# A fused attention and gMLP block on one core: a prologue written out as one order, z2's normalisation dealt out anew among the engines, weights split earlier, and loads paced

## The chip, the cores and the metric

The kernel runs on one core of one Trainium2 chip. A core has five engines with a queue of instructions each: TensorE (PE: matrix products; PEld is its loading of weights), VectorE (DVE), ScalarE (ACT: functions of one argument, such as exp, tanh, square, copy), GpSimd (POOL) and SyncE (SP), which here only issues DMA transfers. Data lie in SBUF (128 partitions) and in PSUM, where TensorE writes. An engine takes the instructions of its queue in order; engines wait for each other through semaphores. The metric is device time in microseconds, the median of several runs.

## The reference

With x of 2048 x 512 and xn = layernorm(x):

```
A:  q, k, v = split(xn @ wqkv)             # 32 heads of 16
    p = softmax(q k^T / 4);  A = concat(p v) @ wo
B:  z  = gelu(xn @ w_in)                   # 2048 x 1792, tanh form
    z1 = z[:, :896];  z2 = layernorm(z[:, 896:])
    g  = w_sp @ z2 + b_sp[:, None]         # w_sp: 2048 x 2048
    B  = (z1 * g) @ w_out
out = x + A + B
```

All is float32. The softmax is exact, with each query's maximum taken off before the exponential.

## The kernel before, in words

**Products.** Dense products are made of three passes in the format fp32r: each operand is split into a high part (a rounded copy) and a low part (the rest), and hi x hi, lo x hi and hi x lo are summed in PSUM. Splitting is a copy (ScalarE or GpSimd) and a subtraction (VectorE or GpSimd). In the main loop a dense slot is a pair of matmuls on the two halves of the array's rows, into the two halves of the PSUM tile `dps`; three further PSUM tiles, `sl[0..2]`, serve the attention and are handed out by `take`.

**Attention.** The 32 heads go in 16 pairs (p), each with 4 groups of 512 queries (c) and 16 tiles of keys (kt): 1024 steps. Each step has a scores product `scores` (L1157), an exponential on ScalarE (`exp`, tile `pf`, 8 buffers), and its part of the product with v (`values`, L1258, in bursts of 8 steps, so 128 bursts). The maxima come from a product of their own, `maxima` (L1171), whose rows VectorE reduces (`max_red`, L872, tile `mm`). After 16 of them, `max_fin` writes the negated maxima through DRAM (`mscr`) into two extra rows of the stacked q (`qst`), so that the scores product itself takes them off. The scores of a group can't start before its 16 maxima have come back. v lies in `vall`; `v_rest` makes its tiles 4 to 15 in pairs.

**The written order and the planner.** The whole program is one instruction stream per engine, written by a planner in Python that keeps a clock for each engine (`T`) with estimated durations. The main loop goes through the strings of `ORDER`: S scores, M maxima, D dense slot, V a burst of values; one string is one cycle and has 24 D. The dense work is a queue of generators: `v_rest`, `qk_rest` (q and k of head groups 1 to 3), `z2_all` (16 tiles), `z1_all` (14 pairs), `spatial` (28 units of 48 slots), `mlp_out`, `attn_out`. After each pair or tile, a "q" holds the queue until the next burst (`hold`), if more than 8 slots were spent. If nothing else can be done, `filler` (L1230) multiplies zeros. Work of ScalarE, VectorE and GpSimd off the main chain is made of tasks with a priority; those of priority 2 on ScalarE and VectorE run inside a window, the time of the burst, or when older than `AGE`. The list `late` holds DMA issues with due times. `room` counts free buffers; of the tag "big" there are 19 tiles of 512 KB.

**The prologue** (before the main loop, L1043 to L1086) is written group by group of 512 rows of x: `norm_x` (statistics on VectorE, L341; scale, L344 to L346; applied by GpSimd, L350), `turn_x` (transposes on TensorE, L356, split by `split`, L242), `qk_first` (q and k of the first four head pairs, L245 to L247, split and stored, then reloaded as stacks by `load_stacks`), and `v_tile` for four tiles of v. The first weights come twice, once by SP for the subtraction (L268) and once by GpSimd's queue as the high part (L262). v's weights are split by GpSimd (L270, L271). Transposed x is stored to `xscr` by GpSimd's queue: groups 0 and 1 in the prologue (L164), 2 and 3 in the main loop (from L158, from `XAT` on, `XBY` apart). The first maxima come after the prologue, once the planner's clock is past `FIRST`.

**z2** (`z2_norm`, L511): per tile of 128 x 896, ScalarE squares (a gelu in tanh form), GpSimd scales (L518) and multiplies (L520), ScalarE takes tanh, GpSimd adds 1 (L524) and multiplies by z (L526), VectorE takes the statistics (two of 448, L533, and one aggregate, L535), GpSimd forms the scale from them (L539 to L544, one column each) and applies it in two parts, hi and lo (L550 to L554), and SP stores them to `z2scr`.

**Weights ahead.** `weight` loads a weight, waits, and splits it on GpSimd (L291, L293). `ahead_of_time` does that for the 7 weights of z1 and 8 of the spatial product and stores the parts to DRAM (`w1scr`, `wsscr`), from where `fetch_parts` brings them back when needed. Both are spawned in `qk_rest`. `z_loader` brings z2's parts for the spatial product.

## Time and profile before

| | us |
|---|---|
| median of 3 runs (lowest, highest) | 1856.94 (1855.68, 1857.37) |
| the profiled execution | 1855.84 |
| its span, first to last instruction | 1853.9 |
| TensorE busy | 1807.5 (97%) |
| VectorE busy | 1440.9 (78%) |
| ScalarE busy | 1189.6 (64%) |
| GpSimd busy | 722.0 (39%) |
| first dense slot of the main loop | 64.91 |
| first scores product | 102.70 |
| first burst of values | 114.70 |

The profile is one execution, taken by the hardware profiler. A row of its timeline has a start, a duration, the engine, the line of the kernel, the operation, what it writes and reads, a count, and in brackets how long the engine had been idle and who released it. Rows of the same kind that follow each other are merged. Matmuls overlap, so the time from one start to the next tells what one costs, not its duration. A group row gives the count, the total busy time, the mean in ns of one, and the idle time before the group's instructions. POOL's spans are rough.

### The profile page before, as it was taken

What the parts mean: (1) busy time and instruction counts of PE and PEld (TensorE: products, weight loads), DVE (VectorE), ACT (ScalarE), POOL (GpSimd) and SP (SyncE); (2) the same over time, 40 slices, a digit from 0 to 9 for tenths busy, and PEclk for the clock granted to TensorE, in tenths of its full rate; (3) what the DMA queues carried; (4) which work ended last, traced back from release to release, by engine and by line L of the source; (5) the groups of instructions that cost most, each with busy time, mean ns of one, the idle gap of its engine ahead of it and who ended that gap; (6) DMA issues with size and microseconds to landing.
All of it is one profiled execution on the core that took longest, in us unless ns stands there. A gap on an engine that the chain in (4) does not pass through costs nothing.

```text
span 1853.9 us, 38030 instructions
## 1 busy us (share of the span) xinstructions
PE 1807.5 (97%) x14778; PEld 1093.5 (59%) x14778; DVE 1440.9 (78%) x1677; ACT 1189.6 (64%) x1292; POOL 722.0 (39%) x808
## 2 busy tenths in 40 slices
PE   6999999999999999999999999999999999999998
PEld 4766566655655565556556665666656556565543
DVE  6578778888888787877878787787778878787883
ACT  2157777687776777666666665666656666565665
POOL 5324342778888777222452135102522240002200
PEclk9999999999999999999999999999999999999999
DMA  7728872533565246656867558565767667575422
GB/s 236 288 93 283 277 238 87 127 91 112 133 217 137 100 119 201 152 160 154 219 171 199 156 180 217 155 146 154 194 164 186 177 173 148 149 175 143 130 86 80
DMA packets 212124, 306.14 MB, mean 165 GB/s; under 512 B 36816, under 2 KB 108048, under 8 KB 209056
## 3 DMA queue, kind: packets, MB, share of 16 engines
q1 hardware_dynamic: 202824, 273.83, 53.8%
q0 software_dynamic: 9120, 29.89, 4.7%
q8 instruction: 116, 1.90, 0.4%
q14 instruction: 64, 0.52, 0.1%
HBM read 193.80 MB, written 109.85 MB: 164 GB/s over the span
## 4 chain that ended last, share of the span: by engine, by line
PE 87%; DVE 5%; DMA 2%; ACT 2%; issue 1%; POOL 1%; SPq 1%; DVEq 0%; ACTq 0%; POOLq 0%
PE dps L1216 35%; PE sl L1258 23%; PE sl L1157 14%; PE sl L1171 12%; DVE mm L872 3%; SPq L134 1%; PE dps L1230 1%; ACT pf L78 1%; DMA zs<-z2scr 1%; POOL wsp L293 0%; DMA wsp_11r<-in_w_spT 0%; PE sl L247 0%; PE sl L246 0%; PE sl L245 0%; PE sl L1016 0%
## 5 line engine op out<-in xcount | busy, mean ns | idle before, releaser
L872 DVE TENSOR_REDUCE mm<-sl 128x2 f32<-128x1024 f32 x1024 | 1223.8, 1222 | 202.2 <-PE sl L1171 195.8
L78 ACT ACTIVATE pf<-sl 128x1024 f32<-128x1024 f32 x1024 | 1041.6, 1026 | 335.1 <-PE sl L1157 298.5
L1258 PE MATMUL sl<-pf,vall 128*32 128x512 f32 x4096 | 467.9, 595 | 1.0 <-DVE on L1006 0.6
L1157 PE MATMUL sl<-qst,kst 50*128 50x512 f32 x2048 | 436.0, 418 | 9.4 <-DVE mm L872 2.9
L1171 PE MATMUL sl<-kst,qst 48*128 48x512 f32 x2048 | 422.1, 405 | 4.5 <-DVE mm L872 2.4
L1216 PE MATMUL dps<-wsp,zs 64*128 64x512 f32 x2352 | 379.0, 392 | 1.6 <-DMA zs<-z2scr 1.5
L1157 PEld LDWEIGHTS sl<-qst,kst 50*128 50x128 f32 x2048 | 194.3, 184 | 221.9 <-issue 79.6
L1258 PEld LDWEIGHTS sl<-pf,vall 128*32 128x32 f32 x4096 | 119.3, 109 | 266.9 <-issue 234.3
L1171 PEld LDWEIGHTS sl<-kst,qst 48*128 48x128 f32 x2048 | 195.1, 185 | 105.0 <-ACT pf L78 52.6
L1216 PEld LDWEIGHTS dps<-wsp,zs 64*128 64x128 f32 x2352 | 226.9, 187 | 39.3 <-DMA zs<-z2scr 2.2
L78 ACT ACTIVATE e<-sl 128x512 f32<-128x512 f32 x64 | 38.3, 598 | 205.2 <-PE sl L1258 198.0
L1280 DVE TENSOR_TENSOR e<-sl,e 128x512 f32<-128x512 f32 x64 | 44.3, 692 | 134.3 <-PE sl L1258 76.3
L778 POOL TENSOR_TENSOR hhl<-z1i,hhl 128x512 fp32r<-128x512 f32 x28 | 36.1, 1297 | 267.1 <-ACT hhl L78 267.0
L1216 PE MATMUL dps<-w,xt 64*128 64x448 f32 x768 | 110.4, 368 | 1.5
L1216 PE MATMUL dps<-wout,hp 64*128 64x512 f32 x672 | 110.5, 393 | 0.0
L923 POOL TENSOR_TENSOR ob<-ob 128x512 f32<-128x512 f32 (+1 forms) x16 | 20.6, 1285 | 195.2 <-DMA ob<-rscr 195.2
L1216 PEld LDWEIGHTS dps<-w,xt 64*128 64x128 f32 x768 | 73.5, 186 | 16.3 <-issue 7.8
L1216 PEld LDWEIGHTS dps<-wout,hp 64*128 64x128 f32 x672 | 65.8, 187 | 9.2
L919 POOL TENSOR_TENSOR ob<-ob 128x512 f32<-128x512 f32 (+1 forms) x16 | 20.6, 1287 | 101.6 <-DMA ob<-escr 100.9
L443 POOL TENSOR_TENSOR qkhl<-qr,qkhl 128x512 fp32r<-128x512 f32 x24 | 30.3, 1282 | 70.4 <-ACT qkhl L78 66.3
L1216 PE MATMUL dps<-wf,zs 64*128 64x512 f32 x336 | 55.5, 393 | 0.1
L1216 PE MATMUL dps<-xnT,wqk 64*128 64x512 f32 x288 | 47.7, 396 | 1.1 <-ACT vall L78 0.4
(289 smaller groups left out, 1688.3 us busy)
## 6 DMA issues: line engine op xcount, KB each, us to landing
zs<-z2scr SPq DMA_DIRECT2D x192, 256.0 KB
escr<-e SPq DMA_DIRECT2D x60, 256.0 KB
hscr<-hhl POOLq DMA_DIRECT2D x28, 512.0 KB, 6.4
qst<-qscr SPq DMA_DIRECT2D x30, 384.0 KB
kst<-kscr SPq DMA_DIRECT2D x30, 384.0 KB
qscr<-qkhl SPq DMA_DIRECT2D x16, 512.0 KB
kscr<-qkhl SPq DMA_DIRECT2D x16, 512.0 KB
xscr<-xnT POOLq DMA_DIRECT2D x16, 512.0 KB, 4.8
```

The costliest lines, as they stand in the source:

```text
L78: return nc.scalar.activation(out, in_, func, **kw)
L134: nc.sync.dma_start(raw(dst), raw(src))
L443: nc.gpsimd.tensor_sub(hl[:, 1, :], raw_, hl[:, 0, :].bitcast(F32))
L778: nc.gpsimd.tensor_sub(hl[:, 1, :], z1, hl[:, 0, :].bitcast(F32))
L872: nc.vector.tensor_reduce(mmax[g][:, :, t, kc], sl[k], AX.X, ALU.max)
L919: nc.gpsimd.tensor_add(both_[rows, 0, :], both_[rows, 0, :], both_[rows, 1, :])
L923: nc.gpsimd.tensor_mul(both_[rows, 0, :], both_[rows, 0, :], both_[rows, 1, :])
L1157: nc.tensor.matmul(sl[k][:, j, :], kst[p % 2][rows, kt * P:(kt + 1) * P], qst[p % 2][rows, c * 512:(c + 1) * 512], start=True, stop=True)
L1171: nc.tensor.matmul(sl[k][:, j, :], qst[p % 2][rows, tt * P:(tt + 1) * P], kst[p % 2][rows, kc * 512:(kc + 1) * 512], start=True, stop=True)
L1216: nc.tensor.matmul(dps[:, bank, :w], lhs, rhs, start=go, stop=stop)
L1258: nc.tensor.matmul(sl[k][cols:cols + VW, 0, :], vpack(kt + r, 2 * p + j), pf[:, j * 512:(j + 1) * 512], start=n % CYC == 0, stop=n % CYC = ...
L1280: nc.vector.tensor_add(e, sl[k][:, 0, :], e)
```

## The change

1. **The prologue is one list of words, `STEPS`,** which the class `First` turns into instructions. Its letters: S statistics, R scale, N apply (a star: the second tile on ScalarE), T transposes, E split of transposed x, Z its store (group 0 only, by SP), WH/WL high and low part of the first weights, Q and F the first q and k (a star: by ScalarE and GpSimd), L load of stacks, B the bias, VH/VL v's weights, V and VE v's first tiles, M and X the first 16 maxima and their reductions. PSUM tiles are handed out in turn (four). The first weights are loaded once and split on the chip; 22 products of zeros (`WARM`) come before the first transposes. The main loop starts with 16 maxima done and `max_fin(0)` spawned; `FIRST` is gone. Groups 1 to 3 of transposed x are stored in the main loop by GpSimd's queue, from 5 us on, 2 us apart.
2. **v's outputs:** of each pair, one is evicted by VectorE instead of ScalarE. The hold after a pair now applies only once all of v is done.
3. **z2:** tanh's +1 and the product with z, with the sum over the row, are one VectorE instruction per half of 448; GpSimd adds the two sums to the negated mean; ScalarE squares z minus its mean with the sum over the row. The statistics, the aggregate and two GpSimd instructions go. `u` is freed after the square. The planner's durations for GpSimd in z2 change.
4. **Weights ahead** are spawned in `v_rest`, at the second pair, all 15 at once, instead of in `qk_rest` in three lots.
5. **Pacing:** `road`, `clear` and `bulk`: a weight load is issued only when the planner's clock has passed the end of the loads before, counted at 1 us each, a fetch of parts or of z2 at 2 us (a z2 part that is needed next goes anyway). x is fetched again for q and k at wider steps (1.5 for 0.5).
6. `AGE` goes from 6 to 9.

```
-FIRST = 7.0
+VAHEAD = 6
-XAT = 8.0
+XAT = 5.0
-AGE = 6.0
+AGE = 9.0
+WARM = 22
+STEPS = (
+    "S00 S01 R00 WH0 N00 WL0 R01 S10 N01* T01 S11 WH1 T03 E03 T00 E01 R10 T02 WL1 E02 E00 R11 N10 N11* Q00 T13 T12 "
+    "T11 F00* S20 VH1* S21 E13 R21 E12 Q01 VH3* T10 N21* S30 R20 E11 E10 Q11 VL1* R30 N20 F01* B VH0 Z03 N30* "
+    "T20 S31 E20 R31 T23 Z02 L0 F11 Z01 E23 N31* Q10 F10 T32 T21 T22 T30 E32 E22 E21 Q20 VH2 L1 T31 VL3 E30 "
+    "T33 Q21 VL0 F20 E31 VL2 M02 E33 M00 Q31 X02 F21 M13 M10 L2 X00 Q30 X13 F31 M03 M01 X10 X03 F30 V3 M22 M12 Z00 "
+    "X01 M23 VE3 X22 V0 VE0 X12 M21 X23 M20 X21 L3 M11 V1 X20 M32 M30 X11 M31 X32 X31 VE1 V2 X30 M33 X33 VE2 "
+)
...
     def weight(out, k, a, spare):
-        yield "C", lambda: raws[0] < DEEP and room["big"] > 1 + spare[0]
+        yield "C", lambda: clear() and raws[0] < DEEP and room["big"] > 1 + spare[0]
+        bulk(1.0)
...
     def fetch_parts(out, k, scr, spare):
-        yield "C", lambda: room["big"] > 1 + spare[0]
+        yield "C", lambda: clear() and room["big"] > 1 + spare[0]
+        bulk(2.0)
...
     def v_out(t, bank):
-        yield "A", ta(512)
-        act(vhead[:, t, :, :DH], dps[:, bank, :].rearrange("p (h d) -> p h d", d=DH), AF.Copy)
+        src = dps[:, bank, :].rearrange("p (h d) -> p h d", d=DH)
+        if bank:
+            yield "D", td(512)
+            nc.vector.tensor_copy(vhead[:, t, :, :DH], src)
+        else:
+            yield "A", ta(512)
+            act(vhead[:, t, :, :DH], src, AF.Copy)
...
+            if t == VAHEAD:
+                for f in range(NF):
+                    owed[0] += 1
+                    spawn(ahead_of_time(f, (f"w1_{f}", w_in[:, f * P:(f + 1) * P], D, ND), w1scr[f], AHEAD), 1)
+                for s in range(KEPT):
+                    owed[0] += 1
+                    spawn(ahead_of_time(s, sp_weights(0, s), wsscr[s], AHEAD), 1)
...
         act(u, u, AF.Tanh, scale=GC)
-        yield "G", 1.2
-        nc.gpsimd.tensor_scalar(u, u, 1.0, 1.0, ALU.add, ALU.mult)
-        yield "G", 2.1
-        nc.gpsimd.tensor_mul(z, u, z)
+        for j, half in enumerate((a, b)):
+            cols = slice(j * 448, (j + 1) * 448)
+            yield "D", 0.63
+            nc.vector.scalar_tensor_tensor(z[:, cols], u[:, cols], 1.0, z[:, cols], ALU.add, ALU.mult, accum_out=half)
+        yield "G", 0.6
+        g.tensor_scalar(m, a, b, -1.0 / FH, ALU.add, ALU.mult)
+        yield "A", ta(FH) + 0.2
+        act(u, z, AF.Square, bias=m, accum_out=square)
         lease("big", 1)
-        for j in range(2):
-            yield "D", 0.62
-            nc.vector.bn_stats(st[:, j, :], z[:, j * 448:(j + 1) * 448])
-        yield "D", 0.1
-        nc.vector.bn_aggr(mv, st)
...
     def z_loader():
         for k in range(len(zparts)):
-            yield "C", lambda: k < zused[0] + 4 and room["big"] > (min(owed[0], ZROOM) if k > zused[0] + 1 and owed[0] else raws[0] > 0)
+            yield "C", lambda: (clear() or k <= zused[0] + 1) and k < zused[0] + 4 and room["big"] > (min(owed[0], ZROOM) if k > zused[0] + 1 and owed[0] else raws[0] > 0)
+            bulk(2.0)
             load_z(k)
...
+        for _ in range(WARM):
+            nc.tensor.matmul(dps[:, 1, :], zeror, brow, start=True, stop=True)
+        first = First(w0r, w0, wvr, wv, braw)
+        for word in STEPS.split():
+            first.step(word)
         steady.append(True)
-        T.update(P=0.0, A=0.0, D=0.0, G=0.0)
+        T.update(P=0.0, A=0.6, D=2.0, G=0.0)
...
-        for g in range(2, NG):
+        for g in range(1, NG):
             for c in range(ND):
-                at(XAT + XBY * (4 * g - 8 + c), nc.gpsimd.dma_start, raw(xscr[g][c]), raw(xnT[g, c]))
+                at(XAT + XBY * (4 * g - 4 + c), keep, g, c)
...
+        spawn(max_fin(0), 0, T["D"])
+        n_st, n_mx, n_pv = 0, 16, 0
...
                 elif it[0] == "q":
-                    hold = spent > 8 and n_pv < N
+                    hold = spent > 8 and n_pv < N and len(vdone) == NT - EARLY
```

More of the change, by code (lines that the diff above doesn't have):

```diff
@@ L247, in mm3, with begin @@
         nc.tensor.matmul(acc, lh, rl, start=False, stop=last)
[L249 removed]
+    def begin(nm, src, n, blocks=1):
         rw = piece(nm + "r").bitcast(F32)[:, 0, :n]
[L253 removed]
+        dst = rw
         if blocks > 1:
@@ L1043, in fused_block @@
         load_x(0)
+        w0r = [begin(*qk_weights(0, a)) for a in range(2)]
         w0 = [piece(f"wqk0_{a}") for a in range(2)]
-        w0r = [begin(*qk_weights(0, a), early=w0[a]) for a in range(2)]
         load_x(1)
@@ L1179, in mx_ok @@
         def mx_ok(t):
-            return n_mx < LEAD and t > FIRST
+            return n_mx < LEAD
         def has_dense(t):
```

240 lines of the change are left out of this document (124 added, 116 removed).

## The prediction

> **What bounds the kernel now.** I read four views in this order: the busy times, stretches by stage, the timeline of the score-times-value bursts (128 of them, one per "cycle"), and the timelines of the opening. The first two, with the group of filler matmuls:
>
> ```profile
> PE 1807.5 (97%) x14778; PEld 1093.5 (59%) x14778; DVE 1440.9 (78%) x1677; ACT 1189.6 (64%) x1292; POOL 722.0 (39%) x808
> ...
> L1230 PE MATMUL dps<-brow,zeror 64*128 64x512 f32 x206 | 39.3, 408 | 0.5 <-ACT z1x L78 0.3
> ...
> 0.00:64.90 64.90, 47.85 (x208) 36.31 (x208) 34.61 (x83) 19.06 (x37) 27.73 (x44) 0.97 0.77 267
> 64.90:133.10 68.20, 63.87 (x516) 44.56 (x516) 50.19 (x52) 24.28 (x30) 23.07 (x29) 1.00 0.42 145
> 133.10:290.70 157.60, 155.17 (x1288) 95.15 (x1286) 126.21 (x141) 116.25 (x134) 63.18 (x62) 1.00 0.78 255
> 290.70:517.30 226.60, 221.42 (x1835) 136.72 (x1834) 187.60 (x232) 166.51 (x185) 161.76 (x190) 1.00 0.42 113
> 517.30:750.70 233.40, 230.17 (x1874) 134.69 (x1874) 186.90 (x215) 167.84 (x190) 183.06 (x214) 1.00 0.50 152
> 750.70:1805.60 1054.90, 1046.77 (x8748) 629.72 (x8748) 839.18 (x935) 670.19 (x690) 263.23 (x270) 1.00 0.64 165
> ```
>
> A row of the second kind is a stretch, its length, then busy time of PE, PEld, DVE, ACT and POOL, clock, DMA share and GB/s. TensorE bounds the kernel. Its idle time is 17.0 us in the opening (64.90 - 47.85), 4.3 in the next stretch, 5.2 in the z2 stage (290 to 517), and 8.1 in the thousand microseconds from 750 on (the spatial stage and the outputs), so there is little to win there. Busy time hides 103 pairs of fillers (206 matmuls of zeros).
>
> ```profile
> 114.70 3.64 PE L1258 MATMUL sl<-pf,vall 128*32 128x512 f32 x32
> 129.51 3.64 PE L1258 MATMUL sl<-pf,vall 128*32 128x512 f32 x32
> 145.04 3.64 PE L1258 MATMUL sl<-pf,vall 128*32 128x512 f32 x32
> ...
> 406.25 3.64 PE L1258 MATMUL sl<-pf,vall 128*32 128x512 f32 x32
> 419.64 3.64 PE L1258 MATMUL sl<-pf,vall 128*32 128x512 f32 x32
> ...
> 517.28 3.64 PE L1258 MATMUL sl<-pf,vall 128*32 128x512 f32 x32
> ...
> 1805.56 2.78 PE L1258 MATMUL sl<-pf,vall 128*32 128x512 f32 x24
> ```
>
> These are the bursts. The second starts at 129.51, the 125th at 1805.56: 123 cycles of 13.63 us. The one from 406.25 ran with no dense work at all, fillers only, and still took 13.39. So a cycle has two limits of the same size, the dense slots on TensorE and the chain of exponentials and maxima. The end therefore sits at "start of the second burst + 126 cycles + tail", as long as the dense pieces keep up with the cycles (a pair or tile of 18 to 24 slots each, one per cycle). The profiled execution took 1855.84 us (span 1853.9); the median of the three runs, 1856.94, is 1.1 above it.
>
> **Part 1, the opening.** Before, TensorE leaves the opening at 64.91, and only then come the first 16 maxima, in 19.62 us of VectorE, and the scores at 102.70:
>
> ```profile
> 4.53 0.69 DVE L341 BATCH_NORM_STATS2 bst<-x 128x6 f32<-128x512 f32 x1 [2.50 <-DMA x<-in_x]
> ...
> 6.05 0.18 DVE L342 BATCH_NORM_AGGREGATE mv<-bst 128x2 f32<-128x6 f32 x1
> 6.60 0.17 DVE L345 RECIPROCAL rs<-rs 128x2 f32<-128x2 f32 x1 [0.36 <-ACT rs L344]
> 6.80 0.16 DVE L346 SCALAR_TENSOR_TENSOR rs<-mv,rs 128x2 f32<-128x2 f32 x1
> ...
> 50.17 1.88 DVE L242 TENSOR_TENSOR xnT<-sl,xnT 128x512 fp32r<-128x512 f32 x3
> ...
> 71.36 19.62 DVE L872 TENSOR_REDUCE mm<-sl 128x2 f32<-128x1024 f32 x17 [8.45 <-PE sl L1171]
> ...
> 48.52 1.04 PE L356 MATMUL sl<-ident,x 128*128 128x128 f32 x8
> ...
> 61.34 0.39 PE L245 MATMUL dps<-qst,xnT 128*128 128x512 f32 x1
> ...
> 63.83 0.39 PE L247 MATMUL dps<-kst,xnT 128*128 128x512 f32 x1
> 64.91 1.43 PE L1216 MATMUL dps<-qst,xnT 64*128 64x512 f32 x10 [0.69 <-ACT vall L78]
> ...
> 102.70 0.41 PE L1157 MATMUL sl<-qst,kst 50*128 50x512 f32 x2
> ...
> 121.22 0.96 PE L1216 MATMUL dps<-xnT,wqk 64*128 64x512 f32 x6 [0.40 <-ACT vall L78]
> ...
> 128.26 1.32 PE L1216 MATMUL dps<-xnT,wqk 64*128 64x512 f32 x10
> ```
>
> After, the written order holds for VectorE: 8 pairs of statistics (4.53 to 6.23, 1.70 each) 13.6; 8 scale steps (6.60 to 6.96) 2.9; 16 low parts of x, 6 of q and k, 2 of the first weights and 3 of v's, 27 of 0.627 (1.88 / 3), 16.9; 16 maxima of 1.154 (19.62 / 17) 18.5; with a small split of the bias, rounded up to 1, together 53. The start at 4.53 is set by the load of x, which stays first in SP's queue, so VectorE is through at 57.5 if it never waits. TensorE has 64 transposes of 0.13 (1.04 / 8), 8.3; 96 + 48 products of 0.227 (63.83 - 61.34 over 11 steps), 32.7; 16 maxima pairs of about 0.23, 3.7: 44.7, from about 10 on, so 55. VectorE is the longer. The 22 warm-up matmuls run while x is on its way, and cost nothing as long as the first normalised halves come later than they end; otherwise at most 22 x 0.227 = 5. The last q and k part must still go out to memory and come back as stacks; maxima of earlier key groups fill that time. I add 5.5 for waits that the order can't hide (ends 0 and 17, the idle time of TensorE in the whole old opening; nearer to 0 because every engine but VectorE has slack here): 16 maxima done at 63 instead of 91. TensorE is free some 1.5 earlier, at 61.5 instead of 64.91, and with 16 maxima already done.
>
> From there to the second burst TensorE took 64.6 us before (64.91 to 129.51). After, some 12 of the 16 maxima pairs are gone from it (12 x 0.227 = 2.7; I let the other four go into running further ahead). So are the q/k products that ran in it: the rows from 121.22 to 128.26 are 46 matmuls, 23 slots of two, 5.2. In the new order no q/k work runs ahead of the second burst, which needs all of v. v's outputs, split between ScalarE and VectorE, may save 1 (ends 0 and 6 x 0.5, one wait like the 0.40 in the row for each pair). That leaves 55.7, so the second burst starts at 117.2: **-12.3**. The 23 slots come back later, in cycles that had fillers. The next cycle, 15.53 before (129.51 to 145.04), should be the mean 13.63: **-2**.
>
> What can eat this is the way of the first maxima to memory and back, for which TensorE waits in its own order:
>
> ```profile
> 122.08 0.61 POOL L291 CAST w<-w_0r 128x512 fp32r<-128x512 f32 x1 [33.97 <-DMA w_0r<-in_w_in]
> ...
> 123.50 1.28 POOL L293 TENSOR_TENSOR w<-w_0r,w 128x512 fp32r<-128x512 f32 x1
> ...
> 184.01 5.82 DMA qst<-mscr
> ...
> 1141.65 10.77 DMA zs<-z2scr
> ...
> 90.00:121.00 31.00, 29.17 (x236) 19.51 (x232) 24.91 (x31) 13.97 (x18) 0.00 (x0) 1.00 0.07 21
> ```
>
> Around 90 to 121 the DMA engines are idle (0.07) and POOL has nothing. The change puts there the 12 stores of x transposed (GpSimd's queue, 2 us apart), 15 weight splits (0.61 + 1.28 us of POOL each) and their loads and stores in SP's queue, where a store that waits for POOL holds up what stands behind it. So the first return of maxima no longer has the road to itself: between 0 and 5.82 (the loaded case above) late; I take **+1**. The same move takes 15 weights out of 133 to 290, where that wait stood in the chain of work that ended last: **-1**.
>
> **Part 2, z2.** Its groups, all in the z2 stretch and a bit beyond:
>
> ```profile
> L526 POOL TENSOR_TENSOR z<-z2u,z 128x896 f32<-128x896 f32 x16 | 33.8, 2110 | 0.3
> ...
> L533 DVE BATCH_NORM_STATS2 zst<-z 128x6 f32<-128x448 f32 x32 | 18.9, 611 | 3.1 <-POOL z L526 3.1
> ...
> L524 POOL TENSOR_SCALAR z2u<-z2u 128x896 f32<-128x896 f32 x16 | 15.0, 940 | 31.7 <-ACT z2u L78 31.5
> L78 ACT ACTIVATE z2u<-z2u 128x896 f32<-128x896 f32 x16 | 15.0, 953 | 3.8 <-POOL z2u L520 3.8
> ```
>
> Per tile POOL loses 2.11 + 0.94 and gains one on a single column: some -2.8. VectorE swaps two statistics (2 x 0.61) and a small aggregate for two products with sums of the same width: even, if nothing holds them up. ScalarE gains one square, 0.95. ScalarE is at 166.5 of 226.6 there and would go to 182; VectorE is at 187.6. POOL is at 161.8 and starts the next stage with a backlog; the cycle from 406.25 without dense work is where it held up new tiles. That cycle's 24 slots are about what the opening pushed back, so I book the relief of POOL against those 23 slots, and the pace of z2 at **0**. Without that cover the 23 slots cost 5.2 at the end.
>
> Against it stands how VectorE and POOL get at the same memory:
>
> ```profile
> 38.63 0.61 POOL L270 CAST kst<-wv3r 128x512 fp32r<-128x512 f32 x1
> ...
> 38.72 0.54 DVE L346 SCALAR_TENSOR_TENSOR rs<-mv,rs 128x2 f32<-128x2 f32 x1
> ...
> L915 DVE TENSOR_TENSOR os<-os x16: 176/181/1032, 818.0 to 1761.8; 128x32 f32<-128x32 f32 x12, 96x32 f32<-96x32 f32 x4
> ```
>
> The tiny operation of 0.16 us took 0.54 when it began under a cast of POOL, and ended at 39.26, just after it (39.24); a sum of 0.18 once took 1.03. The new products read u and z, both from the same memory, while POOL is busy 71% of the stage. Each can wait from 0 to 2.11 (POOL's longest operation). Ends for 16 tiles of two: 0 and 67. I stay near 0, at 0.25 a product of which half is on the path, because the planner puts this work into the burst, when VectorE has no maxima: 32 x 0.125 = **+4**. The Trainium skill, "SBUF — State Buffer", section "Who interferes with whom", says that a VectorE instruction with two inputs from SBUF contends with a GpSimd instruction that reads SBUF, and that the later one blocks for the whole of the other. The trace's row agrees. By that rule each product pays POOL's remaining operation, which is the second rival.
>
> **Part 3, pacing.** Weights go out at least 1 us apart, z2 parts 2 us. In the spatial stage a z2 part took 10.77 to land with TensorE waiting behind it. Ends: -8 (all of TensorE's idle time from 750 on) and +6 (one more return as late as the 5.82). The bytes moved stay the same, so I take **-2**. The longer age (9 for 6) shifts work that fills gaps anyway: 0, with the same 6 as its bad end if exponentials wait behind it. POOL enters z1 with less of a backlog; TensorE idles 3.2 from 517 to 750: **-2**.
>
> Sum: -12.3 - 2 + 1 - 1 + 4 - 2 - 2 = -14.3, on 1856.9 (the profiled execution would be 1.1 under that): **1842**.
>
> **The rivals.** (a) Only TensorE's own time counts: 3.4 us earlier at the hand-over plus 16 maxima pairs (3.7), so -7, and the 23 slots reappear at the end instead of in filler cycles: 1850. For it: TensorE idles 8 us in the last thousand. Against: the cycle without dense work. (b) Slower: VectorE's two-input products wait on POOL in z2, on the path. With a whole long operation each, 2 x 2.11 a tile, 16 tiles, 67 us, of which 60% on the path, 40; so -18.3 without the +4 becomes +22: 1879. It decides from 18.3 / 16 = 1.1 us a tile on. For it: VectorE is 83% busy there. Against: the burst hides some, and statistics had the same place. At 1.2 to 1.5 a tile it ends at 1858 to 1863. (c) More: z2 cycles fall from 13.88 (406.25 to 517.28, eight of them) to the 13.39 of the one without dense work (16 x 0.49 = 8) and the landing stalls go (6 more): 1828. For it: POOL no longer holds tiles up; against: ScalarE's extra square. (d) The change does not do what it says: stalls on returns and loads in the new opening use up its gain, 1857.
>
> **How the numbers follow.** My forecast has 0.42 (its own range 1834 to 1848), (a) 0.20, (c) 0.18, (b) 0.15, (d) 0.05. A difference under 0.2% (3.7 us) can't be told from none here. Faster takes the first three, 0.80; same 0.05; slower 0.15. The range runs from 1826, just under (c), to 1857, which takes in (d) and leaves (b) out above.
>
> **What would show it.** Right: the 16th maximum ends near 63, scores start near 75, the second burst near 117, no cycle in z2 with fillers only. Wrong in part 1: a wait of TensorE on the returned maxima, or VectorE idle over 6 us before 63. Wrong in part 2: products over 1 us in the z2 groups, cycles there above 14.3. The whole is wrong if the second burst comes early but the last one does not.

## The result, and the profile after

The changed kernel takes 1848.95 us (median of 5 runs, 1847.42 to 1851.89) against 1856.94 before (5 runs, 1855.68 to 1858.39). The ratio is 0.9964, 95% interval 0.9952 to 0.9975, which is 7 us; the two medians alone lie 8 us apart. So it is faster by 7 to 8 us, where 15 had been forecast. The profiled execution took 1848.92 us, its span 1847.1.

Timeline of the changed kernel, TensorE's bursts (line 1258 before is line 1313 now):

```profile
94.29 3.64 PE L1313 MATMUL sl<-pf,vall 128*32 128x512 f32 x32
124.82 3.64 PE L1313 MATMUL sl<-pf,vall 128*32 128x512 f32 x32
138.68 3.64 PE L1313 MATMUL sl<-pf,vall 128*32 128x512 f32 x32
...
287.30 3.64 PE L1313 MATMUL sl<-pf,vall 128*32 128x512 f32 x32
...
509.12 3.64 PE L1313 MATMUL sl<-pf,vall 128*32 128x512 f32 x32
...
741.80 3.64 PE L1313 MATMUL sl<-pf,vall 128*32 128x512 f32 x32
...
1130.96 3.64 PE L1313 MATMUL sl<-pf,vall 128*32 128x512 f32 x32
1149.41 3.64 PE L1313 MATMUL sl<-pf,vall 128*32 128x512 f32 x32
...
1799.08 3.64 PE L1313 MATMUL sl<-pf,vall 128*32 128x512 f32 x32
```

These are the 1st, 2nd, 3rd, 14th, 30th, 47th, 76th, 77th and 125th burst; before, they started at 114.70, 129.51, 145.04, 294.50, 517.28, 750.70, 1139.47, 1156.17 and 1805.56. So the lead over the kernel before is 20.4, 4.7, 6.4, 7.2, 8.2, 8.9, 8.5, 6.8 and 6.5 us. The first burst is far ahead, the second, which needs all of v, only 4.7; z2 and z1 add 1.7; the spatial stage gives 2.4 back.

Three stretches of the changed kernel, the opening, z2 and the spatial stage, with the bounds of the same bursts as in the prediction (length, then busy time of PE, PEld, DVE, ACT, POOL, then clock, DMA share, GB/s), and with them the busy line and the two groups of products of zeros:

```profile
PE 1809.0 (98%) x14774; PEld 1094.1 (59%) x14774; DVE 1445.7 (78%) x1700; ACT 1210.1 (66%) x1329; POOL 673.9 (36%) x778
...
0.00:68.90 68.90, 60.12 (x268) 43.99 (x268) 52.66 (x101) 25.44 (x48) 20.17 (x31) 0.95 0.71 249
...
287.30:509.10 221.80, 215.63 (x1812) 136.23 (x1810) 185.27 (x248) 178.29 (x209) 142.17 (x201) 1.00 0.46 127
...
741.80:1799.10 1057.30, 1049.20 (x8753) 629.35 (x8752) 841.00 (x939) 670.72 (x690) 263.51 (x270) 1.00 0.63 165
...
L1285 PE MATMUL dps<-brow,zeror 64*128 64x512 f32 x180 | 34.4, 410 | 1.2 <-ACT z1x L86 0.7 <-DVE z L457 0.3
L1134 PE MATMUL dps<-brow,zeror 128*128 128x512 f32 x22 | 7.8, 531 | 2.0 <-POOL brow L104 2.0
```

The hand-over to the main loop, the start of the first dense slot, is at 68.90, later than the 64.91 of before, and not at the 61.5 forecast, though now with 16 maxima done. TensorE's idle time fell from 46.4 (1853.9 - 1807.5) to 38.1 (1847.1 - 1809.0), the fillers from 39.3 to 34.4, and 7.8 of warm-up products came in.

The rows of the opening where it was lost: SyncE's queue, VectorE's split of one q, TensorE's waits and the two of VectorE that follow from them; then three stretches, whose clock is the number after the five engines:

```profile
28.26 0.89 SPq L142 DMA_DIRECT2D xscr<-xnT  x2
30.08 1.12 SPq L142 DMA_DIRECT2D kst<-kscr  x1
30.12 0.69 DVE L244 TENSOR_TENSOR qkhl<-sl,qkhl 128x512 fp32r<-128x512 f32 x1 [0.39 <-ACT qkhl L86]
31.72 1.15 SPq L142 DMA_DIRECT2D kst<-kscr  x1
33.96 0.95 SPq L142 DMA_DIRECT2D xscr<-xnT  x1
35.01 2.24 SPq L142 DMA_DIRECT2D qscr<-qkhl  x2
41.17 0.32 SPq L142 DMA_DIRECT2D qst<-qscr  x1
44.16 0.47 PE L1100 MATMUL sl<-kst,qst 48*128 48x512 f32 x1 [2.46 <-DMA kst<-kscr]
45.52 1.22 PE L1100 MATMUL sl<-kst,qst 48*128 48x512 f32 x3 [0.89 <-DMA kst<-kscr]
46.35 1.23 DVE L1105 TENSOR_REDUCE mm<-sl 128x2 f32<-128x1024 f32 x1 [4.81 <-PE sl L1100]
52.51 1.23 DVE L1105 TENSOR_REDUCE mm<-sl 128x2 f32<-128x1024 f32 x1 [3.21 <-PE sl L1100]
68.90 1.66 PE L1271 MATMUL dps<-qst,xnT 64*128 64x512 f32 x12 [0.57 <-DVE mm L1105]
...
30.00:35.00 5.00, 4.99 (x31) 4.03 (x30) 4.37 (x7) 3.19 (x7) 0.00 (x0) 1.00 1.01 339
...
45.00:50.00 5.00, 4.48 (x11) 3.15 (x12) 2.95 (x3) 0.00 (x0) 0.00 (x0) 0.50 0.75 284
50.00:55.00 5.00, 5.00 (x20) 3.43 (x19) 2.49 (x3) 0.60 (x1) 0.00 (x0) 0.82 0.58 216
```

The q of group 1 was split at 30.81, but its store left only at 35.01: three stores of transposed x stand ahead of it in SyncE's queue, and with the DMA engines full (a share of 1.01) two loads of stacks took 1.12 and 1.15 to issue. Its load back could be issued only at 41.17. TensorE waited 3.35 (2.46 + 0.89) for the stacks, and then ran at half the clock; VectorE stood 4.81 and 3.21 behind it.

### The profile page after: what moved, and what is told of

It is laid out like the page before. It is cut to its first block, busy times and chain, and to the rows that moved or that the text cites. A ratio compares the mean times of both kernels' runs of the same rounds, so it can differ in the third digit from the quotient of the medians.

```text
span 1847.1 us, 38060 instructions
## 1 busy us (share of the span) xinstructions
PE 1809.0 (98%) x14774; PEld 1094.1 (59%) x14774; DVE 1445.7 (78%) x1700; ACT 1210.1 (66%) x1329; POOL 673.9 (36%) x778
## 4 chain that ended last, share of the span: by engine, by line
PE 87%; DVE 5%; DMA 3%; POOL 1%; issue 1%; SPq 1%; ACT 1%; DVEq 0%; POOLq 0%; ACTq 0%
PE dps L1271 35%; PE sl L1313 23%; PE sl L1212 14%; PE sl L1226 12%; DVE mm L823 4%; SPq L142 1%; PE dps L1285 1%; DMA zs<-z2scr 1%; POOL wsp L288 1%; PE sl L247 1%; PE sl L249 0%; PE sl L248 0%; ACT pf L86 0%; DMA wsp_10r<-in_w_spT 0%; PE sl L967 0%
## 5 line engine op out<-in xcount | busy, mean ns | idle before, releaser
L823 DVE TENSOR_REDUCE mm<-sl 128x2 f32<-128x1024 f32 x1008 | 1208.0, 1222 | 200.5 <-PE sl L1226 193.0
L1226 PE MATMUL sl<-kst,qst 48*128 48x512 f32 x2016 | 414.9, 404 | 4.5 <-DVE mm L823 2.9
L1271 PE MATMUL dps<-xnT,wqk 64*128 64x512 f32 x288 | 48.1, 394 | 0.3
## 6 DMA issues: line engine op xcount, KB each, us to landing
xt<-xscr SPq DMA_DIRECT2D x64, 128.0 KB
```

The costliest lines, as they stand in the source:

```text
L823: nc.vector.tensor_reduce(mmax[g][:, :, t, kc], sl[k], AX.X, ALU.max)
L1226: nc.tensor.matmul(sl[k][:, j, :], qst[p % 2][rows, tt * P:(tt + 1) * P], kst[p % 2][rows, kc * 512:(kc + 1) * 512], start=True, stop=True)
L1271: nc.tensor.matmul(dps[:, bank, :w], lhs, rhs, start=go, stop=stop)
```

## The experiments

Each run is told by its ratio to the time before (1 is no change, 0.001 is 1.9 us; an interval is 0.0009 to 0.0017 to either side) and by stage lengths between bursts of its profile, which is one execution:

| run | ratio | 2nd burst at | 2nd-14th | 14th-30th (z2) | 30th-47th (z1) | 47th-125th | 125th-end |
|---|---|---|---|---|---|---|---|
| before | 1 | 129.5 | 165.0 | 222.8 | 233.4 | 1054.9 | 48.3 |
| changed | 0.9964 | 124.8 | 162.5 | 221.8 | 232.7 | 1057.3 | 48.0 |
| after_again | 0.9966 | 125.6 | 162.4 | 221.8 | 232.7 | 1059.6 | 48.1 |
| e1 stores late | 0.9945 | 118.4 | 162.4 | 221.7 | 233.5 | 1059.5 | 48.2 |
| e6 zeros in the wait | 0.9960 | 123.0 | 162.3 | 221.7 | 232.5 | 1057.8 | 48.0 |
| e8 tiles shifted | 0.9968 | 124.1 | 162.5 | 221.8 | 232.6 | 1059.4 | 48.1 |
| e2 v by ScalarE | 0.9974 | 122.1 | 162.8 | 221.6 | 232.6 | 1059.3 | 48.0 |
| e4 no pacing | 0.9952 | 124.8 | 162.4 | 221.8 | 233.8 | 1055.5 | 48.0 |
| e3 old z2 | 1.0009 | 126.6 | 162.5 | 228.7 | 238.0 | 1052.1 | 49.4 |
| e12 age 6 | 1.0024 | 124.8 | 162.4 | 232.9 | 233.4 | 1058.1 | 49.1 |
| e5 old place of weights, x fetched 0.5 apart | 1.0016 | 125.5 | 174.9 | 221.6 | 232.7 | 1057.1 | 48.7 |
| e9 before + prologue | 1.0065 | 123.6 | 169.4 | 223.3 | 242.3 | 1053.2 | 54.3 |
| e11 before + prologue + z2 | 1.0051 | 124.1 | 167.7 | 233.5 | 232.4 | 1055.1 | 48.0 |
| e10 before + z2 | 1.0039 | 130.1 | 166.3 | 230.2 | 232.7 | 1054.7 | 49.6 |
| e13 before + age 9 | 1.0055 | 128.0 | 164.7 | 225.2 | 237.6 | 1049.8 | 59.1 |
| e15 before + z2 + age 9 | 0.9950 | 130.6 | 164.9 | 220.9 | 231.4 | 1049.1 | 50.0 |
| e14 = e1 + e2 | 0.9933 | 117.8 | 162.8 | 221.6 | 232.6 | 1060.6 | 49.7 |
| e7 = e1 + e2 + e4 | 0.9923 | 117.4 | 162.9 | 221.6 | 233.0 | 1059.9 | 48.6 |
| e17 landing 10 | 0.9982 | 123.2 | 162.4 | 221.8 | 232.8 | 1052.3 | 59.2 |
| e16 = e7 + landing 10 | 0.9940 | 119.1 | 162.9 | 221.5 | 233.5 | 1053.0 | 59.1 |

### The opening: stores, clock, tiles, v

e1 takes four words, the stores of transposed x, from their places to the end of the list, and starts the main loop's stores 1 us later:

```
-XAT = 5.0
+XAT = 6.0
-    ... VH0 Z03 N30* "  / "... T23 Z02 L0 F11 Z01 E23 ..." / "... M12 Z00 "
-    "X01 ... M33 X33 VE2 "
+    "X01 ... M33 X33 VE2 Z03 Z02 Z01 Z00 "
```

> The changed kernel (1848.95) with the four stores of x transposed moved behind the whole written order in SP's queue, and the first of the stores on GpSimd's queue 1 us later, so that it does not run ahead. Theory (the round trip of q and k to memory takes longer because other stores fill the DMA engines): qscr's store lands in some 3.3 us instead of 5.1, TensorE's wait before the maxima of key group 1 falls from 3.35 to under 1, its clock stays at 1.00, the 16th maximum ends at 64 instead of 68.9, the second burst starts at 119 instead of 124.8, and the whole takes 1843 to 1845. Rival (the round trip is that long by itself): the wait stays over 2.5 us, the burst moves by less than 1, and the time is 1848 to 1850.

SyncE's queue, the hand-over and the same stretch in e1:

```profile
30.31 0.41 SPq L142 DMA_DIRECT2D kst<-kscr  x1
31.80 1.53 SPq L142 DMA_DIRECT2D qscr<-qkhl  x2
36.63 0.32 SPq L142 DMA_DIRECT2D qst<-qscr  x1
...
62.44 0.73 PE L1271 MATMUL dps<-qst,xnT 64*128 64x512 f32 x4 [0.56 <-DVE mm L1105]
...
45.00:50.00 5.00, 5.00 (x26) 3.10 (x24) 3.69 (x5) 1.20 (x2) 0.00 (x0) 1.00 0.78 284
```

The outcome is the theory's, the way only in part: the load of the stacks starts 4.5 earlier (36.63 for 41.17), but 3.2 of it is that the store left earlier (31.80 for 35.01), its place in the queue, and only 1.3 the faster round trip that the theory named. TensorE has no wait there, the clock is full, the hand-over is 6.5 earlier and the second burst at 118.37. The ratio of 0.9945 is 3.5 us better than the changed kernel.

e6 fills the wait with work that changes nothing:

```
             acc = self.take("m", kc, t)
+            if (kc, t) == (1, 3):
+                for _ in range(12):
+                    nc.tensor.matmul(acc[:, 0, :], zeror, brow, start=True, stop=True)
```

> The changed kernel with 12 products of zeros into the PSUM tile of the maxima product that waits (key group 1, query tile 3), so that TensorE is busy during most of that wait; nothing else differs. Theory (the low clock after the wait is caused by the wait and costs 2.4 us): the clock of the stretch from 45 to 55 is 1.00 instead of 0.50 and 0.82, the 12 products behind the wait take 2.7 us instead of 5.1, and the second burst comes 2 to 2.5 earlier: 1846.5. Rival (VectorE sets the order, TensorE has slack there): the clock is full and the second burst stays within 0.5 of 124.8, 1849.

The clock from 40 to 55 is 1.00 throughout, and the second burst comes 1.9 earlier. Not all of it is the clock's: in this profile the stacks' load was also issued 0.75 earlier (40.42 for 41.17), which leaves some 1.1 for the clock, where 2.4 had been expected. In the whole time 0.7 (0.9960 for 0.9964) can't be told from nothing.

e8:

```
-            ..., self.turn = {}, {}, {}, [], [], 0
+            ..., self.turn = {}, {}, {}, [], [], 2
```

> The changed kernel with the four PSUM tiles of the prologue handed out with another start, so that the last maxima product does not lie in the tile that the first dense slot needs. Theory (the hand-over waits for the last reduction only because of that tile): the first dense slot starts 1.2 to 1.6 us earlier (67.4 instead of 68.90), the second burst as much, 1847.5. Rival (the first dense slots only gain a wait later): the slot starts earlier, the second burst stays within 0.5 of 124.8.

A miss for both: the first dense slot starts 0.7 earlier (68.24) and the second burst too. The last reduction then held back a maxima product ahead of the slot by the same 0.57, and the clock behind the wait was higher in this profile (0.67 from 45 to 50, for 0.50), which may be all of the 0.7. So the tile was not the reason.

e2, in `v_out`, so that ScalarE evicts both tiles:

```
-        if bank:
+        if False:
             yield "D", td(512)
```

> The changed kernel with both outputs of each pair of v on ScalarE, as before the change. Theory (the two evictions write parts of one tile and are held apart, so that the split makes each pair later instead of earlier): TensorE's idle time at the pairs of v falls from 0.95, 0.49, 1.41 and 1.41 to 0.5 to 0.7 each, and the second burst starts 1 to 2.5 earlier than 124.8: 1847. Rival (the prediction's: the split saves 1): the burst is 1 later, 1850.

Rows of the changed kernel at the first pair, then of e2:

```profile
75.55 0.60 ACT L86 ACTIVATE vall<-dps 128x512 f32<-128x512 f32 x1 [7.76 <-PE dps L1271]
76.18 0.69 DVE L426 COPY vall<-dps 128x512 f32<-128x512 f32 x1 [1.71 <-ACT vall L86]
76.92 1.66 PE L1271 MATMUL dps<-qst,xnT 64*128 64x512 f32 x12 [0.95 <-DVE vall L426]
```

```profile
75.23 0.96 PE L1271 MATMUL dps<-qst,xnT 64*128 64x512 f32 x6 [0.71 <-ACT vall L86]
```

VectorE's copy waits for ScalarE's, since both write the tile `vall`: the split runs one after the other, and TensorE waits 0.95 instead of 0.71 (and 1.41 instead of 1.18 at the last two pairs). The second burst is 2.8 earlier, of which 1.5 lies ahead of the hand-over (67.43), where the clock stayed at 1.00 in this profile; 1.3 is v's. From the hand-over to the second burst it is 54.63 here, 54.60 in e14 and 54.59 in e7, against 55.92 in the changed kernel and 55.93 in e1. The ratio, 0.9974, shows no gain.

### z2 and the age

Five runs, each with only the named parts changed: e3 puts the old `z2_norm` into the changed kernel, with its planned durations and with five small buffers for six; e10 puts the new one into the kernel before; e12 is the changed kernel with the old age, e13 the kernel before with the new one; e15 is e10 with the new age.

```
-AGE = 9.0
+AGE = 6.0
```

(that is e12; e13 and e15 have it the other way round.)

> The changed kernel with z2's normalisation as it was before the change (the products, the +1 and the scale from VectorE's statistics on their old engines, with the old planned durations); five small buffers instead of six, for want of room. Prediction: the change of z2 costs 4 and gains nothing, so 1845. Theory from the two traces (the new products wait little, a mean of 0.645 us against a least of 0.612, and the z2 stage got 0.7 shorter): 1849 to 1852, z2 stage (14th to 30th burst) 222 to 224. A third way (GpSimd holds new tiles up as before): a cycle without dense work comes back, 1853.

> The kernel before with only z2's normalisation changed (products and sums by VectorE, squares by ScalarE, the new planned durations). The changed kernel with the old z2 took 1.0009, so there the new z2 was worth 8 us. Theory (GpSimd holds z2's tiles up in any case): z2 stage from the 14th to the 30th burst 219 to 221 instead of 222.8, the whole 1848 to 1852. Rival (only the new opening brings z2's stage to GpSimd's limit; in the old kernel q and k products fill those gaps): stage within 1 of 222.8, the whole 1855 to 1858. The prediction's +4: 1861.

> The changed kernel with the age back at 6, nothing else. Theory (with the new z2 the longer age keeps its VectorE and ScalarE work in the bursts; with 6 it comes due between the maxima and exponentials): the z2 stage from the 14th to the 30th burst takes 229 to 231 instead of 221.8, as in the two runs with the new z2 and the age of 6 (230.2, 233.5), and the whole 1855 to 1858. Rival (the prediction's: the age shifts work that fills gaps anyway): stage within 1 of 221.8, the whole 1848 to 1850.

> The kernel before with the age at 9 instead of 6, nothing else. Theory (with the old z2 the longer age delays GpSimd's input, as in the run with the old z2 and the age of 9, 228.7): z2 stage 226 to 229 instead of 222.8, the whole 1859 to 1864. Rival (a longer age is good for both): stage under 222, the whole 1853 to 1856. The prediction's 0: within 1.

> The kernel before with the new z2 and the age of 9, old prologue and the rest. The new z2 with the age of 6 took 1.0039. Theory (the two belong together): z2 stage 221 to 222 instead of 230.2, the whole 1854 to 1857, no better than before, so that the gain of the whole change is the opening's. Rival (the stage gets long again because q and k products still lie in it or the weights come late): 225 or more, 1859 and over.

On the old opening: old z2 with age 6 is 1, the new z2 alone 1.0039, the age alone 1.0055, both 0.9950. Each alone costs 7 to 10 us, both together gain 9. The changed kernel shows the same: without the new z2 1.0009, without the age 1.0024. For e15 the expectation of no gain was wrong: it is as fast as the whole change. None of the five theories had the time right: e3, e10, e12 and e13 came out 7, 12, 4 and 4 us above theirs, e15 6 below, and the 10 us of e13 do not lie where its theory put them (2.4 more in z2, 4.2 in z1, and an end 10.8 longer behind a spatial stage 5.1 shorter). The groups in the z2 stretch, of the changed kernel and of e12:

```profile
L1226 PE MATMUL sl<-kst,qst 48*128 48x512 f32 x256 | 53.3, 408 | 2.0 <-DVE mm L823 2.0
L1285 PE MATMUL dps<-brow,zeror 64*128 64x512 f32 x18 | 4.5, 499 | 0.5 <-DVE z L457 0.3
...
L481 DVE SCALAR_TENSOR_TENSOR z<-z2u,z 128x448 f32<-128x448 f32 x32 | 20.0, 645 | 5.8 <-ACT z2u L86 5.8
...
L481 DVE SCALAR_TENSOR_TENSOR z<-z2u,z x32: 612/619/1422, 317.4 to 539.2; 128x448 f32<-128x448 f32 x32
```

```profile
L1226 PE MATMUL sl<-kst,qst 48*128 48x512 f32 x256 | 53.3, 407 | 6.0 <-DVE mm L823 4.7 <-ACT pf L86 1.3
L1285 PE MATMUL dps<-brow,zeror 64*128 64x512 f32 x76 | 14.2, 435 | 0.9 <-ACT z L86 0.6
...
L481 DVE SCALAR_TENSOR_TENSOR z<-z2u,z 128x448 f32<-128x448 f32 x32 | 22.6, 744 | 4.7 <-ACT z2u L86 4.7
```

With age 6, the maxima products wait 6.0 for VectorE and ScalarE instead of 2.0, and 76 fillers run instead of 18. That fits z2's work coming between the maxima once it counts as old; with 9 it waits for the burst. The same rows show a second cost, the new products themselves: 0.744 on average for 0.645. Two rows of e10, the age of 6 on the old opening:

```profile
313.20 2.11 POOL L520 TENSOR_TENSOR z2u<-z2u,z 128x896 f32<-128x896 f32 x1
313.23 2.56 DVE L530 SCALAR_TENSOR_TENSOR z<-z2u,z 128x448 f32<-128x448 f32 x1
```

The product that began 0.03 after GpSimd's took 2.56. Products over 1 us number five of 32 in e10 and in e12, one in the changed kernel, none in e15; that is 4 to 5 us of VectorE in e10 and e12 (32 times what the means of 0.756 and 0.744 lie above the least of 0.61). That the age decides is shown; the way is argued from these rows, and how much of the loss belongs to each of the two was not separated. With the old z2 and age 9 (e3), another wait appears on VectorE's queue:

```profile
449.19 1.15 DVE L484 BATCH_NORM_STATS2 zst<-z 128x6 f32<-128x448 f32 x2 [4.25 <-POOL z L477]
```

The statistics stand in front of the maxima's reductions, which follow at 450.25, and wait 4.25 for GpSimd's product: that cycle took 17.19. The new z2 has no such place, since what VectorE waits for there comes from ScalarE.

### The prologue alone, and the place of the weights

e9 is the kernel before with the new prologue and hold rule; e11 has the new z2 as well; e5 is the changed kernel with the weights' splitting in `qk_rest` again, as before, and with x fetched for q and k 0.5 apart again instead of 1.5:

```
     def v_rest():
-            if t == VAHEAD:
-                ... spawn(ahead_of_time(f, ...w1scr[f], AHEAD), 1) ... spawn(ahead_of_time(s, ...wsscr[s], AHEAD), 1)
     def qk_rest():
+        for f in range(NF):
+            ... spawn(ahead_of_time(f, ...w1scr[f], AHEAD), 1)
...
-                    fetch_xnT((g + 1) % NG, 1.5)
+                    fetch_xnT((g + 1) % NG, 0.5)
...
+                if (g, m) in ((3, 1), (0, 1)):
+                    ... spawn(ahead_of_time(s, ...wsscr[s], AHEAD), 1)
```

> The kernel before with the new prologue alone: z2, the place of the weights' splitting, the pacing, the age and v's outputs are as before; only the rule for the hold while v is unfinished comes along, and three times five small buffers instead of six. Theory (the opening carries the gain, all else adds up to nothing): second burst near 123, the whole 1848 to 1850. Rival (without the relief of GpSimd in z2 and the earlier weights the work pushed back from the opening comes due in z2): second burst near 123, the z2 stage from the 14th to the 30th burst 226 or more with cycles of fillers only, and the whole 1853 to 1856.

> The kernel before with the new prologue, the hold rule and the new z2, but weights, pacing, age and v's outputs as before. The prologue without the new z2 took 1.0065. Theory (the two belong together, and the earlier weights and the rest add little): 1846 to 1850, z2 stage 222. Rival (the weights' splitting, still beside q and k, keeps GpSimd behind and holds back the maxima's return, as the 19.26 cycle at the tenth burst of the run without the new z2 showed): that cycle again over 18, the whole 1853 to 1860.

> The changed kernel with the 15 weights split beside q and k again, in three lots, as before the change; pacing, age, v's outputs and z2 stay as changed. Theory (the earlier place takes waits out of the q and k stage): the cycle at the tenth burst is longer than 13.8 by up to 5, the whole 1851 to 1855. Rival (the place does not matter, as the prediction's +1 and -1): stages within 1, 1848 to 1850.

The early burst alone is worth less than nothing: 1.0065, with 169.4 from the 2nd to the 14th burst and 242.3 in z1 (the rival had put the loss into z2, where it is not). With the new z2 (e11) the tenth burst's cycle is again 18.01, and the z2 stage, 233.5, is as long as with the age of 6 (232.9 in e12). The times missed again: e9 came out 13 us above its rival, e11 8 above its rival, whose long cycle it has, and e5 6 above its theory. e5 shows the first of these places, a cycle of 26.07 instead of 13.8 at the tenth burst; two pieces of its chain, TensorE's wait and two rows of SyncE's queue:

```profile
228.28 7.12 DMA qscr<-qkhl
235.41 11.39 DMA qst<-mscr
...
246.84 1.17 PE L1212 MATMUL sl<-qst,kst 50*128 50x512 f32 x2 [9.16 <-DMA qst<-mscr]
...
217.97 7.93 SPq L142 DMA_DIRECT2D wsscr<-wsp  x3
225.99 0.40 SPq L142 DMA_DIRECT2D mscr<-ms  x1
```

SyncE's queue stands for 7.93 in the stores of split weights, and behind them the maxima go to memory and come back 11.39 after their load was issued, with the DMA engines full (a share of 1.04 from 235 to 247). TensorE waits 9.16 for them. With the new prologue the weights would fall on this return; moving them beside v, together with the wider steps for x, takes 12.4 out of that stretch (174.9 for 162.5). That is larger than the whole gain; the prediction had -1. Loads of x stand in the same queue there, so how much of the 12.4 is the weights' alone is not shown. And the kernel before had no such wait (its tenth cycle took 13.78): the move prevents a cost of the new opening more than it takes one out of the old.

### Pacing and the boundary in the spatial stage

e4 has the first of these edits; e14 is e1 with e2, and e7 is both with e4. e17 is the changed kernel with the second edit, e16 is e7 with it.

```
     def clear():
-        return clock() >= road[0]
+        return True
...
-LOADZ = 5.0
+LOADZ = 10.0
```

after_again is the changed kernel once more.

> The changed kernel itself once more, beside the three runs below and on their chip. It tells how far one profile of the same instructions differs from another: stage times within 0.3%, the second burst within 1 of 124.8, the long cycle near 1131 again 18 to 18.5 (before 16.70). If TensorE's clock after the wait near 45 is not 0.50 again, the low clock there is not fixed by the order of the instructions.

> The changed kernel without the pacing: loads of weights and of parts go out as soon as there is room, as before the change. Theory (pacing costs in the spatial stage what the trace lost there, 2.4 from the 47th burst to the 125th): the cycle at the 76th burst falls from 18.45 to under 16.8, the stage from the 47th to the 125th burst takes 1055 instead of 1057.3, and the whole 1846.5. Rival (the prediction's: pacing spares late landings, 2): the stage takes 1059 and the whole 1851.

> The changed kernel with the stores of x transposed behind the written order and both outputs of v on ScalarE, pacing kept; with pacing off as well it took 0.9923. Theory (pacing has a cost of 2): 1844.5 to 1846, long cycle at the 76th burst 18 to 19.5. Rival (pacing is worth nothing here, the length of that cycle is an accident of where the loads fall): 1841 to 1844.

> The changed kernel with three things together: the stores of x transposed behind the written order (measured alone at 0.9945 of the time before), both outputs of v on ScalarE, and no pacing (0.9952 alone; the changed kernel 0.9964 and 0.9966). Theory (the forecast's shortfall is the waits of the opening, which the stores caused, v's outputs and the pacing): second burst at 117 to 118, the cycle at the 76th burst under 16.8, stage from the 47th to the 125th burst 1055.5, the whole 1841 to 1843. Rival (what the opening gains beyond 8 us is given back, because the dense work becomes the limit): second burst at 117 to 118, but the 125th no earlier than 1794, and the whole 1845 to 1847.

> The changed kernel with one planned duration changed: the landing of a z2 part is planned at 10 instead of 5, so the planner does other work on TensorE while the part is on its way (the trace shows 10.9 at the group boundary near 1140). Theory (the spatial stage gave back 2.4 because TensorE stood waiting there and then ran at a low clock): the cycle at the 76th burst takes under 16.5 instead of 18.45, with a clock of 1.00, the stage from the 47th to the 125th burst 1055 instead of 1057.3, and the whole 1846 to 1847. Rival (the time lost there is only spread: fillers instead of a wait, the same slots still to be done): the cycle is shorter, the stage within 1 of 1057.3, the whole 1848 to 1850.

> The best run so far (stores behind the order, both outputs of v on ScalarE, no pacing: 0.9923) with the landing of a z2 part planned at 10 instead of 5. Theory: its cycle of 21.34 at the 76th burst falls under 16.5, the stage from the 47th to the 125th burst from 1059.9 to 1055, the whole to 1838 to 1840. Rival (the slots pushed out of the opening have to be done in any case, so that the stage stays long): 1842 to 1845.

The cycle after the 76th burst, where the spatial product goes to its next group: one row of the kernel before, two of the changed one.

```profile
1151.47:1154.47 3.00, 2.50 (x18) 1.83 (x18) 0.83 (x2) 1.00 (x1) 0.36 (x1) 1.00 0.87 236
```

```profile
1142.96:1145.96 3.00, 2.19 (x9) 1.57 (x11) 0.14 (x1) 0.00 (x1) 0.81 (x1) 0.68 0.87 236
1145.96:1148.96 3.00, 3.00 (x22) 2.37 (x21) 1.77 (x2) 2.04 (x2) 0.00 (x0) 0.75 0.15 44
```

Both wait for a z2 part here, 1.48 before and 1.76 after; only the second loses the clock. The lost clock is not the whole of it, though: e4 waits 2.14 here, keeps a clock of 1.00, and its cycle is still longer than before. The cycle took 16.70 before, 18.45 and 19.25 in the two profiles of the changed kernel, 17.75 in e4, 19.86 in e14, 21.34 in e7, 16.31 in e11, 15.57 in e10, and 13.5 to 14.3 in e3, e9, e13 and e15. Pacing is not what rules it: without it the cycle is shorter in e4 and longer in e7, and 0.9923 (0.9911 to 0.9935) against 0.9933 (0.9920 to 0.9947) is no difference. Between two profiles of the same kernel the stage from the 47th to the 125th burst differs by 2.3, so the 2.4 given back there is hardly more than that.

Planning with the real landing time takes the wait away (13.70 in e17) and the stage is 5 shorter, but the end is 11 longer. The last two stretches of e17, then the last of the changed kernel, whose spatial stage is shown above:

```profile
740.16:1792.43 1052.27, 1042.89 (x8662) 619.44 (x8660) 838.93 (x936) 671.85 (x690) 263.47 (x270) 1.00 0.62 163
1792.43:1851.60 59.17, 51.99 (x408) 23.83 (x406) 20.50 (x26) 25.21 (x27) 0.00 (x0) 1.00 0.36 117
```

```profile
1799.08:1847.10 48.02, 42.62 (x328) 16.66 (x326) 17.16 (x23) 25.22 (x27) 0.00 (x0) 1.00 0.21 78
```

That is 91 matmuls fewer in the stage (8662 for 8753), 80 more behind the attention. Dense work that a cycle does not take is paid at the end. Both expectations of a gain fell: e17 takes 0.9982 and e16 0.9940, each more than without the change, though the cycle and the stage came out as short as expected.

e7 is the fastest of all: 1843.43 against 1858.26 before in the same runs, 0.9923, and better than the changed kernel by 7 to 8 us. Its time came close to the theory's 1841 to 1843, but not by the theory's way: the second burst is where it should be (117.41), while the cycle at the 76th burst took 21.34 and the stage 1059.9, so that the 125th burst stands at 1794.7, as its rival had it. That agreement is luck.

## Why the prediction was wrong

The sign was right, the size not. (The sum, -14.3 on 1856.9, is 1842.6; it was put down as 1842, which changes nothing.) The terms against the bursts:

| term | forecast | in the traces |
|---|---|---|
| second burst | -12.3 | -4.7 |
| next cycle | -2 | -1.7 |
| first maxima's return | +1 | 0 (first scores at 80.85, without a wait) |
| q/k stage's stall gone | -1 | -0.8 (rest to the 14th burst) |
| z2, port waits and pace | +4 | -1.0 |
| z1 | -2 | -0.7 |
| pacing, spatial stage | -2 | +2.4 |
| end | 0 | -0.3 |

**The step that failed is "I add 5.5 for waits that the order can't hide ... because every engine but VectorE has slack here".** The term came out at 11.4 (68.85 less the 57.5 without waits). The range given there, 0 to 17, holds it; the choice near 0 was wrong. The work itself was counted right: VectorE was busy 52.66 up to the hand-over, for a sum of 53. The 16th maximum ended at 68.85 instead of 63, and TensorE was free at 68.90 instead of 61.5. The sign named for part 1, VectorE idle over 6 us, came true in one place (4.81 + 3.21). I had counted VectorE and TensorE to the instruction, but not SyncE's queue, which carries the stores of transposed x ahead of the q and k that TensorE waits for. Without them the hand-over is at 62.44 (e1), and with v's eviction undone as well the second burst is at 117.84 (e14) and 117.41 (e7, without pacing too), against a forecast of 117.2. This step is worth the whole shortfall: the second burst lacks 7.6, and the other terms are off in both directions and add up, by cancelling, to what was forecast (-2.1 for -2.0). "May save 1" for v's split had the wrong sign: it costs 1.3. The step from the hand-over to the second burst came out right, 55.92 for 55.7, although this term of it had the wrong sign, so in part by luck.

**The prices of z2, the age and the weights were wrong one by one, and cancelled.** The +4 for z2 is right in kind for the new z2 with the old age (e10, +7 us), and the age, which I let "shift work that fills gaps anyway: 0", turns it into a gain of 9. Its bad end, +6, was argued for the exponentials; alone the age costs 10 (e13), most of it behind z2. The weights' move, -1, with the wider steps for x, is worth 12 in its stretch once the opening is new. Rival (b) was rightly held small, and even the 0.25 a product in the forecast was too much for the changed kernel: the products took 0.645 on average against a least of 0.612, with a single worst of 1.42. By the Trainium skill, "SBUF — State Buffer", section "Who interferes with whom", each could have waited for a whole GpSimd operation. The 2.56 of e10 beside a GpSimd product of 2.11 agrees, but with the age of 9 only one product of 32 was so caught. The sign named for part 2, cycles above 14.3 in z2, says nothing: the longest is 14.84 now and was 14.72 before. Rival (b) had a mechanism that exists, at a size, 40 us, that no run shows.

**Rival (a) gave nearly the right time, 1850, by a wrong way.** The hand-over is not 3.4 earlier but 4.0 later, and the 23 slots pushed out of the opening seem to have come back where I had put them, in fillers, not at the end: the z2 stage had 56 filler matmuls before and 18 after, in a stage 1.0 shorter, and the whole kernel 206 and 180; the end is no longer than before (48.0 for 48.3). But "123 cycles + tail" holds only while the dense work keeps up, and e17 shows how closely it does: what the cycles leave is paid behind the attention.

**What stays open.** e15, without any of the new opening, is as fast as the whole change. Its spatial stage is 5.8 shorter than the kernel before's, with no wait at the boundary of the groups (13.49); z2 and z1 together are only 3.9 shorter. Why the boundary falls well there and badly (17.75 to 21.34) in the changed kernel and in those of its variants that keep the new z2 and the planned landing, and whether that is all, was not settled; planning for the landing did not help. Whether e7 would gain further with e15's alignment was not tried.

## What to carry to other kernels

Price the parts of a planned schedule together: here two changes that cost 7 and 10 us alone gained 9 in company, so a term of the sum is worth something only for the neighbours it was read with. When an opening is rewritten, count the DMA queue like an engine, issue by issue: a store that nobody waits for still stands ahead of one that somebody does. And an earlier start is worth only what it takes from TensorE's idle time and fillers; work moved out of it must be followed to where it is paid.

## What the runs showed of the hardware

TensorE's clock falls after waits much shorter than any stage, and not always after the same one. Waits of 1.17 + 0.31 us near the 76th burst left it at 1.00, 1.28 + 0.35 (e1) gave 0.74 and 1.34 + 0.42 gave 0.68, each in the 3 us that hold the second wait; but 1.62 + 0.52 (e4) left it at 1.00, so the length of the wait alone does not decide. In the opening the same order of instructions gave 0.50 (2.46 + 0.89 of waiting), 0.60 (2.48 + 0.66) and, in e2, 1.00 (1.91 + 0.67). The 12 products behind the wait then start 0.43 apart instead of 0.23. The Trainium skill, "TensorE: Matmul & The Clock Gate", section "Part 1: The HAM clock gate (the "warmup" mystery)", says that the gate closes after an idle window of about 3.4 us, that the window runs freely, and that the cost so varies from run to run. The variation agrees; the waits that lost the clock here add up to less than that window, 1.63 in e1, and there the measurement decides.

Some single DMA issues on SyncE's queue took longer with the DMA engines full: two loads of `kst` from 30 to 33 took 1.12 and 1.15 us (a share of 1.01 from 30 to 35), against 0.30 and 0.41 for the same two in e1 (0.47 from 29.4 to 31.2). A load between them took 0.42, so it does not hold for every issue.

VectorE's products with two inputs in SBUF stood behind GpSimd when they began just after one of its instructions: 2.56 us instead of 0.62 beside a product of 2.11 (e10).
